# Block-sparse attention with a routed expert layer: the second pair's chunk 0 last, V's tiles loaded as needed, K in 1536-byte pieces, early dispatch over six steps

## The chip, the cores and the metric

The kernel runs on one core of one Trainium2 chip. Times are microseconds on the device. The median of 3 runs of the kernel before is 666.29 us (665.82 to 667.43). A profile is one execution of the program taken by the hardware profiler. Its times count from the first instruction, and "span" is the time to the last one.

The engines' names in the profile: PE is TensorE's matrix multiplication and PEld its loading of weights, DVE is VectorE, ACT is ScalarE, POOL is GpSimd, SP is SyncE, which only issues DMA here. PEq, DVEq and the like are sequencers. L511 is line 511 of the kernel before.

## The reference

There are two stages. The first is BigBird attention: 4 sequences of 768 tokens, 8 heads of width 64, float32. The keys are split into blocks of 32 tokens. A query block sees its own block and the two next to it, the first and the last block, and three sampled ones; the first and last query block see everything.

```python
scores = scale * np.matmul(q, k.transpose(0, 1, 3, 2))
mask = np.abs(blk_i - blk_j) <= window
mask = mask | (blk_i == 0) | (blk_j == 0) | (blk_i == n_blocks - 1) | (blk_j == n_blocks - 1)
for qb in range(n_blocks):
    for kb in sampled_blocks[qb]:
        mask[qb * block:(qb + 1) * block, kb * block:(kb + 1) * block] = True
scores = np.where(mask, scores, -1000000000.0)
attn = softmax(scores)                 # over the keys
attn_out = np.matmul(attn, v)
```

The second stage takes the 3072 attention rows of width 512 as `x`, sends each to one of 8 experts by the cosine of the row and the expert's embedding, and runs that expert's two layers:

```python
logits = xn @ en.T / tau               # rows of x and of expert_emb at unit length
expert_idx = np.argmax(logits, axis=1)
for e in range(8):
    mask = expert_idx == e
    h = np.maximum(x[mask] @ w1[e], 0.0)          # 512 to 1024
    out[mask] = gate_w[mask, None] * (h @ w2[e])  # 1024 to 512
```

## The kernel before

**Chunks and steps.** A sequence is cut into 6 chunks of 128 tokens, shifted by one block, so that chunk 0 holds the last block and the first three, and with them the sequence's two global query blocks. Two sequences form a pair; a pair-chunk is the same chunk of both. The loop in `attention_fast` (L1308) runs 25 steps. `TURNS` (L56) gives the chunk of each step, `n`, and `place` (L384) its sequence and chunk number: `n` from 0 to 11 belong to the first pair, from 12 to 23 to the second, and chunk 0 comes first in each pair. In step `s` the chunk `now` gets its scores (`score_near`, `score_far`). The chunk of the step before, `last`, is weighted with V (`weigh_near`, `weigh_far`) and divided (`normalize`). The one before that, `past`, is turned (`turn_x`) and gives logits (`chunk_logits`). The queries of the chunk `after` are turned (`turn_q`) and its sampled keys copied together (`gather_k`, one third on DVE and two thirds on POOL).

**Chunk 0** has half the near and half the far scores of another chunk. Its global rows need in addition `score_ends` (four times, one per pair of heads) and `weigh_ends`, which read all keys and all six V tiles of the sequence. They run in the step after the chunk's scores.

**Keys.** K comes in 16 groups (4 sequences by 4 pairs of heads). `load_k` (L412) fetches a group with two DMAs, each of 768 runs of 256 bytes, into one of 5 buffers. `turn_k` (L485) makes six transposes on PE into a PSUM tile of a ring of two, and one copy of 128 x 768 moves them to `kt`, on DVE for even groups and ACT for odd ones. Groups 8 to 15, of the second pair, are turned in steps 10, 11 and 12 (`turning`, L1303), and loaded in the steps that `keys_at` names.

**Values.** Six tiles `vt` hold V of a pair, and the second pair's overwrite the first's, in the steps that `values_at` names. `stack` (ACT) and `near_v` and `stack_ends` (POOL) copy what lies near from them. The sampled blocks come by `gather_v` from DRAM, 12 DMAs of 128 KB per pair-chunk (6 for chunk 0), into a ring of two tiles.

**SP's order.** All of these loads are issued by SP, one after the other, and a DMA whose buffer isn't free holds up all behind it. `fetch_all` (L464) puts the loads of a step between its gathers. The write of a finished pair-chunk's rows to `x_dram` (L808) is issued by SP too, at the start of a later step; the rows lie in three slots, so the write of pair-chunk `b` must land before `normalize` can begin pair-chunk `b + 3`.

**Routing and early dispatch.** `after_step` (L1211) hangs pieces of work on later steps, in their first half (0) or second half (1). For each pair-chunk it is `route`. Once the first two sequences are done, `dispatch_early` sorts their tokens into 5 expert tiles, mostly in small DVE operations. Its 18 calls run in steps 17, 18 and 19, three in each half. In step 20 the first tile's rows are gathered (`fetch_rows`), in steps 20 to 23 the first pieces of its weights are loaded.

**Experts.** `expert_tiles` works 23 tiles of 128 tokens, each with 4 MB of weights, in about 14 us of PE time. `dispatch_late` sorts the remaining tokens on DVE during the second tile, and `spread_slots` (L919) uses the constant `spread`. The first dispatch and the constants (`build_consts`, `build_tokens`) are set up in step 0.

Of the kernel before, what the change touches and what calls it, by code (L numbers as in the profile page):

```python
# [20 lines left out]
P = 128  # L21
# [32 lines left out]
DUO = 2  # L54
# [43 lines left out]
def build_consts(k):  # L98
    nc, pool = k.nc, k.const
    k.ones = pool.tile([P, P], F32, name="ones")  # L100
    nc.vector.memset(k.ones, 1.0)

    groups = k.ident.rearrange("p (g t) -> p g t", g=NG)
    k.spread = pool.tile([P, NG, NG, BLK], F32, name="spread")
    nc.vector.tensor_copy(out=k.spread, in_=groups.unsqueeze(2).broadcast_to([P, NG, NG, BLK]))
# [24 lines left out]
def build_tokens(k, shifted):  # L130

    nc, pool = k.nc, k.const
    tok = pool.tile([P, NT], I32, name="tok")
    pattern = [[-S * DUO, B // DUO], [-P, NC], [-S, DUO]] if shifted else [[-S, B], [-P, NC]]
    nc.gpsimd.iota(tok, pattern=pattern, base=N + BLK * shifted, channel_multiplier=-1)
    if shifted:
        first = tok.rearrange("p (a c i) -> p a c i", c=NC, i=DUO)[:, :, 0]
        nc.vector.tensor_scalar(out=first[0:BLK], in0=first[0:BLK], scalar1=-S, scalar2=None, op0=ALU.add)
    part = pool.tile([P, 2, NT], I32, name="tok_part")
    nc.vector.tensor_scalar(out=part[:, 0], in0=tok, scalar1=6, scalar2=None, op0=ALU.arith_shift_right)  # L140
    nc.vector.tensor_scalar(out=part[:, 1], in0=tok, scalar1=63, scalar2=None, op0=ALU.bitwise_and)
    k.tok = pool.tile([P, 2, NT], F32, name="tok_f")
    nc.vector.tensor_copy(out=k.tok, in_=part)
# [238 lines left out]


def place(n):  # L384

    a, rest = divmod(n, DUO * NC)
    c, i = divmod(rest, DUO)
    return DUO * a + i, c, i

# [13 lines left out]
def load_q(k, s, i=None):  # L403

    a, c = divmod(s, NC)
    if ("q", s) not in k.raw:
        k.raw["q", s] = k.ld.tile([P, DUO, H, D], F32, name="qraw", tag="qraw", bufs=2)
    t, src = in_pair(k.raw["q", s], i), of_seq(k.q, a, i)
    return [(t[rows], src[lo:lo + rows.stop - rows.start]) for rows, lo in pieces(c)]


def load_k(k, g):  # L412

    b, j = divmod(g, NPAIR)
    k.raw["k", g] = t = k.kld.tile([P, NC, 2, D], F32, name="kraw", tag="kraw", bufs=5)
    return [(t[:, :, h], k.k[b, 2 * j + h].rearrange("(c p) d -> p c d", p=P)) for h in range(2)]

# [12 lines left out]
def stack(k, s, i=None):  # L430

    st, c = k.st_ring[s % 2], s % NC
    for half in (1,) if c == 0 else (0, 1):
# [21 lines left out]
def gather_v(k, s, i=None):  # L455

    a, c = divmod(s, NC)
    t, src = k.vg_ring[s % 2], of_seq(k.v, a, i)
# [16 lines left out]
def near_v(k, s, some, i=None):  # L475

    c = s % NC
    for g in blocks_of(c):
# [6 lines left out]
def turn_k(k, g):  # L485
# [270 lines left out]
def route(k, b):  # L756
# [48 lines left out]
    a, c = divmod(b, NC)  # L805
    dram = k.x_dram[DUO * S * a:DUO * S * (a + 1), :].rearrange("(i s) w -> s i w", i=DUO)
# [404 lines left out]
def after_step(n, b):  # L1211
# [12 lines left out]
    if DUO * (b + 1) == EARLY * NC:  # L1224
        n.dispatching = partial(next, dispatch_early(n), None)
        plan += [(s + 4 + i // 6, i // 3 % 2, n.dispatching) for i in range(18)]
        s += 7
        plan += [(s, 0, partial(fetch_rows, n, 0))]
        n.first_weights = fetch_weights(n, 0, 0, 4)
        plan += [(s + i, 1, partial(next, n.first_weights)) for i in range(4)]  # L1230
        plan += [(s + 3, 1, partial(prepare, n, 0))]
    return [(min(when, NCH), part if when <= NCH else 1, what) for when, part, what in plan]


def attention_fast(n, ctx):
# [6 lines left out]
    n.ld, kv, n.qp, n.gp, n.pp = pool("ld", 1), pool("kv", 1), pool("qp", 2), pool("gp", 2), pool("pp", 2)  # L1242
    n.kld = brief = right.enter_context(n.tc.tile_pool(name="brief", bufs=1, side="right"))
    n.setup = setup.enter_context(n.tc.tile_pool(name="setup", bufs=1))
# [392 lines left out]
```

## Time and profile before

| | |
|---|---|
| median of 3 runs | 666.29 us |
| profiled execution's own time | 670.42 us |
| its span | 668.7 us |
| PE busy | 616.0 us, 92% |
| DVE, ACT, POOL busy | 233.5, 140.8, 243.8 us |
| attention, up to the first expert matmul | 302.8 us |
| DMA packets | 187,599; 148,008 of them under 512 bytes |
| mean granted PE clock | 0.955 |

The page cuts the span into 40 slices of 16.7 us; a digit is a busy share in tenths, and PEclk the granted clock in tenths. In a list of instructions the last bracket is the idle time of the engine before it and what ended that. A wait is given as its sum, the number of times and the longest. The chain of waits is followed back from the last instruction, so what stands in it set the end. A line of SP is the issue of a DMA[...].

### The profile page before, as it was taken

To read this page: it belongs to the slowest core of one execution; us is meant where nothing else is said; L and a number is where in the kernel's file an instruction comes from. 1 tells how busy PE (TensorE), PEld (TensorE's weight loads), DVE (VectorE), ACT (ScalarE), POOL (GpSimd) and SP (SyncE) were. 2 spreads that over 40 slices of the span, in tenths; PEclk is the share of its full clock that TensorE was granted. 3 is DMA by queue.
4 is the path that set the end of the run, shared out by engine and by line. 5 is a ranking of instruction groups with operands and counts; after the bars stand their busy time and mean duration, and the time that the engine had idled before them with its cause. 6 is when DMAs were issued, how large, how long until landed. Compare 5 with 4: busy or idle time off the path is not lost.

```text
span 668.7 us, 18349 instructions
## 1 busy us (share of the span) xinstructions
PE 616.0 (92%) x7496; PEld 480.2 (72%) x7496; DVE 233.5 (35%) x739; ACT 140.8 (21%) x285; POOL 243.8 (36%) x461
## 2 busy tenths in 40 slices
PE   6778996498799988999999999999999999999995
PEld 4667986387699887877777776675666765766773
DVE  3552472365334766642851122111121211121210
ACT  1533453154255534530000000000000001000000
POOL 1626264133362544521113433344333343433333
PEclk9897999699599977989999999999999999999999
DMA  9976999699857996839999999999899998999711
GB/s 170 178 145 143 140 165 182 158 170 190 156 90 98 158 141 102 190 131 314 391 396 398 407 397 398 365 321 330 313 411 392 408 374 310 406 399 397 287 49 32
DMA packets 187599, 170.57 MB, mean 255 GB/s; under 512 B 148008, under 2 KB 148136, under 8 KB 184690
## 3 DMA queue, kind: packets, MB, share of 16 engines
q1 hardware_dynamic: 180194, 155.35, 81.2%
q0 software_dynamic: 5216, 13.43, 5.6%
q8 instruction: 61, 1.00, 0.7%
q10 hardware_dynamic: 2096, 0.52, 0.5%
q14 instruction: 32, 0.26, 0.1%
HBM read 156.65 MB, written 12.90 MB: 254 GB/s over the span
## 4 chain that ended last, share of the span: by engine, by line
PE 82%; DVE 5%; SPq 5%; DMA 4%; issue 2%; ACT 1%; POOL 0%; DVEq 0%; POOLq 0%
PE hp L1142 25%; PE yp L1155 24%; PE av L622 8%; PE dps L567 5%; PE yp L710 4%; PE ac L542 3%; DMA kraw<-in_k_dram 3%; PE ac L545 2%; SPq L470 2%; PE xg_ps L506 2%; PE hp L1187 2%; PE yp L1207 2%; SPq L472 2%; PE xg_ps L699 2%; DVE xt L701 1%
## 5 line engine op out<-in xcount | busy, mean ns | idle before, releaser
L1142 PEld LDWEIGHTS hp<-xgt,w 128*128 128x128 f32 x1472 | 167.8, 192 | 10.3 <-issue 10.2
L1142 PE MATMUL hp<-xgt,w 128*128 128x128 f32 x1472 | 169.1, 275 | 0.0
L1155 PE MATMUL yp<-w,h 128*128 128x512 f32 x368 | 161.9, 592 | 0.0
L1155 PEld LDWEIGHTS yp<-w,h 128*128 128x128 f32 x368 | 68.1, 190 | 76.5 <-issue 72.0
L1066 POOL DMA_INDIRECT xg<-x_dram,quarter x88 | 89.2, 1014 | 32.3 <-issue 27.1
L1168 POOL DMA_INDIRECT out_dram<-y,slot_l x20 | 20.5, 1023 | 156.0 <-DVE y L1167 156.0
L1145 ACT ACTIVATE h<-hp 128x512 f32<-128x512 f32 x23 | 13.7, 597 | 284.0 <-PE hp L1142 254.9
L1149 DVE TENSOR_SCALAR h<-hp 128x512 f32<-128x512 f32 x23 | 15.9, 691 | 146.4 <-PE hp L1142 140.0
L482 POOL COPY vg<-vt 32x1040 f32<-32x1040 f32 (+1 forms) x45 | 43.2, 960 | 62.4 <-PE av L622 60.3
L524 POOL COPY kg<-kt 128x128 f32 x176 | 43.2, 291 | 57.4 <-ACT kt L495 45.3
L542 PE MATMUL ac<-qt,kt 128*64 128x128 f32 x352 | 48.7, 296 | 2.1 <-DVE qt L511 2.1
L567 PEld LDWEIGHTS dps<-qt,kg 128*64 128x64 f32 x1408 | 49.0, 143 | 1.6 <-POOL vg L482 1.5
L567 PE MATMUL dps<-qt,kg 128*64 128x64 f32 x1408 | 47.9, 228 | 1.3 <-DVE kg L524 1.3
L545 PE MATMUL ac<-qt,kt 128*64 128x256 f32 (+1 forms) x192 | 48.1, 399 | 0.8 <-ACT kt L498 0.8
L622 PE MATMUL av<-st,pac 128*64 128x65 f32 x704 | 33.0, 239 | 15.7 <-DVE x L799 15.7
L511 DVE COPY qt<-xg_ps 64x512 f32<-64x512 f32 x48 | 33.0, 688 | 40.9 <-PE xg_ps L506 40.6
L542 PEld LDWEIGHTS ac<-qt,kt 128*64 128x64 f32 x352 | 43.2, 152 | 3.1 <-ACT st L434 1.9
L1167 DVE TENSOR_SCALAR y<-yp,gate 128x512 f32<-128x512 f32 x20 | 15.0, 751 | 84.9 <-PE yp L1155 72.8
L622 PEld LDWEIGHTS av<-st,pac 128*64 128x64 f32 x704 | 27.5, 150 | 16.5 <-issue 16.0
L572 ACT ACTIVATE pd<-dps,bias 128x256 f32<-128x256 f32 x88 | 34.7, 474 | 17.2 <-PE dps L567 17.1
L622 PE MATMUL av<-vg,pd 128*32 128x65 f32 x1408 | 31.9, 234 | 0.8 <-issue 0.8
L622 PEld LDWEIGHTS av<-vg,pd 128*32 128x32 f32 x1408 | 24.2, 117 | 9.0 <-issue 8.6
(229 smaller groups left out, 631.0 us busy)
## 6 DMA issues: line engine op xcount, KB each, us to landing
w<-in_moe_w_dram SPq DMA_DIRECT2D x52, 2048.0 KB
vg<-in_v_dram SPq DMA_DIRECT2D x114, 128.0 KB
kraw<-in_k_dram SPq DMA_DIRECT2D x32, 192.0 KB
x_dram<-x SPq DMA_DIRECT2D x10, 516.0 KB
qraw<-in_q_dram SPq DMA_DIRECT2D x9, 512.0 KB
w<-in_moe_w_dram SPq DMA_DIRECT2D x8, 512.0 KB
vt<-in_v_dram SPq DMA_DIRECT2D x10, 256.0 KB
vt<-in_v_dram SPq DMA_DIRECT2D x5, 512.0 KB
```

Of the source, the lines that this page charges most:

```text
L482: k.nc.gpsimd.tensor_copy(out=k.vg_ring[s % 2][NRAND * BLK:P, g, which(i)], in_=k.vt[m][rows, which(i)])
L511: k.nc.vector.tensor_copy(out=t[rows, :, h], in_=ps[rows])
L524: copy(out=t[:, :, g, s * BLK:(s + 1) * BLK], in_=kt[:, :, bass.ds(shift, BLK)])
L542: nc.tensor.matmul(out[0:D, j, half], lhsT=kt[:, j, at:at + D], rhs=qt[:, j, :, D * half:D * (half + 1)], start=True, stop=True)
L545: nc.tensor.matmul(out[D:P, j, half:2].rearrange("p f h t -> p h f t"), lhsT=kt[:, j, S:S + D], rhs=qt[:, j, :, D * half:P].rearrange("p h ...
L567: nc.tensor.matmul(out[D * r:D * (r + 1), NG * j + g], lhsT=kg[:, j, g, D * r:D * (r + 1)], rhs=qt[:, j, :, cols], start=True, stop=True)
L572: nc.scalar.activation(e[:, :, g].rearrange("p j h t -> p j (h t)"), out.rearrange("p (j g) h t -> p j g (h t)", g=NG)[:, :, g], ACT.Exp, ...
L622: k.nc.tensor.matmul(av[lanes, h // NPAIR, h % NPAIR * P:h % NPAIR * P + D + 1], lhsT=lhsT, rhs=rhs, start=first[0], stop=last, skip_group ...
L710: k.nc.tensor.matmul(ps[:, 0:E], lhsT=xt[:, j], rhs=k.en[:, j, :], start=(j == 0), stop=(j == ND - 1))
L1066: k.nc.gpsimd.indirect_dma_start(out=x[:, g], out_offset=None, in_=quarters, in_offset=bass.IndirectOffsetOnAxis(ap=k.quarter[:, g, t:t + ...
L1142: nc.tensor.matmul(hp[:, f, :], lhsT=w1[:, d, (f0 + f) * P:(f0 + f + 1) * P], rhs=xt[:, d, :], start=(d == 0), stop=(d == ND - 1))
L1155: nc.tensor.matmul(yp, lhsT=h[:, f, :], rhs=w2[:, f, :], start=(f == 0), stop=(f == NF - 1))
```

## The change

There are four edits, and what they need around them.

1. `pair_chunk` replaces the division of a pair-chunk's number: the second pair works its chunks in the order 1, 2, 3, 4, 5, 0. Loads, gathers, `stack`, `near_v` and the writes use it, and the token numbers are made pair-chunk by pair-chunk (12 small iotas).
2. `load_k` takes six consecutive tokens per partition, so that a group is one DMA of 256 runs of 1536 bytes. `turn_k` transposes two tokens of one head at a time, and four copies of 64 x 384 put the tokens back in order; their output has a stride of six elements. There are 6 K buffers instead of 5. For the room, the tiles `pb` move to another pool, and `spread` is made in `dispatch_late`.
3. The second pair's K and V tiles get other steps. At the start, q of the second sequence goes ahead of its V tiles, and four of these go behind a gather.
4. The 18 calls of the early dispatch run in steps 16 to 21, one in the first half and two in the second; the first rows are gathered in step 22.

```diff
@@ build_tokens
     if shifted:
-        first = tok.rearrange("p (a c i) -> p a c i", c=NC, i=DUO)[:, :, 0]
-        nc.vector.tensor_scalar(out=first[0:BLK], in0=first[0:BLK], scalar1=-S, scalar2=None, op0=ALU.add)
+        for s in range(NS):
+            a, c = pair_chunk(s)
+            at = tok[:, DUO * s:DUO * (s + 1)]
+            nc.gpsimd.iota(at, pattern=[[-S, DUO]], base=N + BLK - S * DUO * a - P * c, channel_multiplier=-1)
+            if c == 0:
+                nc.vector.tensor_scalar(out=at[0:BLK], in0=at[0:BLK], scalar1=-S, scalar2=None, op0=ALU.add)
...
+def pair_chunk(s):
+
+    a, at = divmod(s, NC)
+    return a, at if a == 0 else (at + 1) % NC
...
 def load_k(k, g):
-    k.raw["k", g] = t = k.kld.tile([P, NC, 2, D], F32, name="kraw", tag="kraw", bufs=5)
-    return [(t[:, :, h], k.k[b, 2 * j + h].rearrange("(c p) d -> p c d", p=P)) for h in range(2)]
+    k.raw["k", g] = t = k.kld.tile([P, 2, NC, D], F32, name="kraw", tag="kraw", bufs=6)
+    return [(t.rearrange("p h c d -> p h (c d)"), k.k[b, 2 * j:2 * j + 2].rearrange("h (p c) d -> p h (c d)", p=P))]
@@ turn_k
-    for c in range(NC):
-        nc.tensor.transpose(ps[:, c // 3, c % 3 * P:(c % 3 + 1) * P], raw[:, c].rearrange("p h d -> p (h d)"), k.ident)
-    copy = nc.scalar.copy if g % 2 else nc.vector.tensor_copy
-    copy(out=kt[:, j, 0:S].rearrange("p (w t) -> p w t", w=2), in_=ps[:, :, 0:3 * P])
+    for h in range(2):
+        for m in range(NC // 2):
+            nc.tensor.transpose(ps[:, h, m * P:(m + 1) * P], raw[:, h, 2 * m:2 * m + 2].rearrange("p e d -> p (e d)"),
+                                k.ident)
+    for h in range(2):
+        to = kt[D * h:D * (h + 1), j, 0:S].rearrange("r (p m e) -> r e m p", m=NC // 2, e=2)
+        for e in range(2):
+            copy = nc.vector.tensor_copy if e == h else nc.scalar.copy
+            copy(out=to[:, e], in_=ps[D * e:D * (e + 1), h, 0:3 * P].rearrange("r (m p) -> r m p", m=NC // 2))
@@ dispatch_late
+    k.spread = p.tile([P, NG, NG, BLK], F32, name="spread")
+    nc.vector.tensor_copy(out=k.spread, in_=k.ident.rearrange("p (g t) -> p g t", g=NG).unsqueeze(2).broadcast_to(
+        [P, NG, NG, BLK]))
@@ after_step
-        plan += [(s + 4 + i // 6, i // 3 % 2, n.dispatching) for i in range(18)]
-        s += 7
-        plan += [(s, 0, partial(fetch_rows, n, 0))]
+        plan += [(s + 3 + i // 3, int(i % 3 > 0), n.dispatching) for i in range(18)]
+        plan += [(s + 9, 0, partial(fetch_rows, n, 0))]
         n.first_weights = fetch_weights(n, 0, 0, 4)
-        plan += [(s + i, 1, partial(next, n.first_weights)) for i in range(4)]
-        plan += [(s + 3, 1, partial(prepare, n, 0))]
+        plan += [(s + 7 + i, 1, partial(next, n.first_weights)) for i in range(4)]
+        plan += [(s + 10, 1, partial(prepare, n, 0))]
@@ attention_fast
-    n.pb_ring = [brief.tile([P, NC, 2, D], F32, name=f"pb{i}") for i in range(2)]
+    n.pb_ring = [n.pp.tile([P, NC, 2, D], F32, name=f"pb{i}", tag=f"pb{i}", bufs=1) for i in range(2)]
...
-    for g in range(5):
+    for g in range(NPAIR):
         fetch_all(n, (), load_k(n, g))
     for m in range(2):
         fetch_all(n, (), load_v(n, 0, m, 0))
+    for g in range(NPAIR, 6):
+        fetch_all(n, (), load_k(n, g))
...
-        if g + 5 < 2 * NPAIR:
-            fetch_all(n, (), load_k(n, g + 5))
-    fetch_all(n, gather_v(n, 1, 0), load_q(n, 0, 1))
-    for m in range(NC):
+        if g + 6 < 2 * NPAIR:
+            fetch_all(n, (), load_k(n, g + 6))
+    fetch_all(n, gather_v(n, 1, 0), load_q(n, 0, 1) + load_q(n, 1, 1))
+    for m in range(2):
         fetch_all(n, (), load_v(n, 0, m, 1))
-    fetch_all(n, gather_v(n, 0, 1), load_q(n, 1, 1))
+    fetch_all(n, gather_v(n, 0, 1), [])
+    for m in range(2, NC):
+        fetch_all(n, (), load_v(n, 0, m, 1))
     fetch_all(n, gather_v(n, 1, 1), [])
...
-    keys_at = {4: (8,), 5: (9,), 6: (10,), 7: (11,), 8: (12,), 10: (13, 14), 11: (15,)}
-    values_at = {4: (0,), 5: (1,), 6: (2,), 8: (3,), 9: (4,), 10: (5,)}
+    keys_at = {3: (8,), 4: (9,), 5: (10,), 6: (11,), 7: (12,), 8: (13,), 10: (14, 15)}
+    values_at = {7: (0,), 8: (1,), 9: (2,), 11: (3,), 13: (4,), 15: (5,)}
```

More of the change, by code (lines that the diff above doesn't have):

```diff
@@ L103, in build_consts @@
     groups = k.ident.rearrange("p (g t) -> p g t", g=NG)
-    k.spread = pool.tile([P, NG, NG, BLK], F32, name="spread")
-    nc.vector.tensor_copy(out=k.spread, in_=groups.unsqueeze(2).broadcast_to([P, NG, NG, BLK]))
     k.mine = pool.tile([P, NG], F32, name="mine")
@@ L133, in build_tokens @@
     tok = pool.tile([P, NT], I32, name="tok")
-    pattern = [[-S * DUO, B // DUO], [-P, NC], [-S, DUO]] if shifted else [[-S, B], [-P, NC]]
-    nc.gpsimd.iota(tok, pattern=pattern, base=N + BLK * shifted, channel_multiplier=-1)
     if shifted:
-        first = tok.rearrange("p (a c i) -> p a c i", c=NC, i=DUO)[:, :, 0]
-        nc.vector.tensor_scalar(out=first[0:BLK], in0=first[0:BLK], scalar1=-S, scalar2=None, op0=ALU.add)
+        for s in range(NS):
[4 more added lines that the diff above has]
+                nc.vector.tensor_scalar(out=at[0:BLK], in0=at[0:BLK], scalar1=-S, scalar2=None, op0=ALU.add)
+    else:
+        nc.gpsimd.iota(tok, pattern=[[-S, B], [-P, NC]], base=N, channel_multiplier=-1)
     part = pool.tile([P, 2, NT], I32, name="tok_part")
@@ L381, in shifts @@
     return k.shift[key]
+def pair_chunk(s):
+    a, at = divmod(s, NC)
+    return a, at if a == 0 else (at + 1) % NC
 def place(n):
-    a, rest = divmod(n, DUO * NC)
-    c, i = divmod(rest, DUO)
-    return DUO * a + i, c, i
+    a, c = pair_chunk(n // DUO)
+    return DUO * a + n % DUO, c, n % DUO
 def of_seq(src, a, i=None):
@@ L403, in load_q @@
 def load_q(k, s, i=None):
-    a, c = divmod(s, NC)
+    a, c = pair_chunk(s)
     if ("q", s) not in k.raw:
@@ L430, in stack @@
 def stack(k, s, i=None):
-    st, c = k.st_ring[s % 2], s % NC
+    st, (_, c) = k.st_ring[s % 2], pair_chunk(s)
     for half in (1,) if c == 0 else (0, 1):
@@ L455, in gather_v @@
 def gather_v(k, s, i=None):
-    a, c = divmod(s, NC)
+    a, c = pair_chunk(s)
     t, src = k.vg_ring[s % 2], of_seq(k.v, a, i)
@@ L475, in near_v @@
 def near_v(k, s, some, i=None):
-    c = s % NC
+    _, c = pair_chunk(s)
     for g in blocks_of(c):
@@ L804, in route @@
         return
-    a, c = divmod(b, NC)
+    a, c = pair_chunk(b)
     dram = k.x_dram[DUO * S * a:DUO * S * (a + 1), :].rearrange("(i s) w -> s i w", i=DUO)
@@ L1242, in attention_fast @@
     n.ld, kv, n.qp, n.gp, n.pp = pool("ld", 1), pool("kv", 1), pool("qp", 2), pool("gp", 2), pool("pp", 2)
-    n.kld = brief = right.enter_context(n.tc.tile_pool(name="brief", bufs=1, side="right"))
+    n.kld = right.enter_context(n.tc.tile_pool(name="brief", bufs=1, side="right"))
     n.setup = setup.enter_context(n.tc.tile_pool(name="setup", bufs=1))
```

## The prediction

> **What bounds the kernel now.** I read first the slices of the page, then the busy time by stretch, then the chain of waits, and last the queues in order of time inside the stretches that lose. A step is one turn of the attention loop; I find its end by the eight logits matmuls (L710), one group per step.
>
> The slices: TensorE is full in the second half (the experts), but holds 4, 6 and 7 in the first, with its clock down.
>
> ```profile
> PE   6778996498799988999999999999999999999995
> PEclk9897999699599977989999999999999999999999
> DMA  9976999699857996839999999999899998999711
> ```
>
> The same by stage. The columns are length, then busy us of PE, PEld, DVE, ACT, POOL, then granted clock, DMA share and GB/s.
>
> ```profile
> 0.00:66.30 66.30, 49.84 (x800) 41.27 (x800) 26.95 (x92) 22.93 (x44) 28.32 (x86) 0.92 0.82 159
> 99.50:132.60 33.10, 17.93 (x403) 16.22 (x401) 10.40 (x39) 8.71 (x19) 9.81 (x28) 0.79 0.90 172
> 140.90:180.00 39.10, 33.15 (x613) 29.25 (x615) 19.13 (x57) 14.19 (x32) 9.66 (x23) 0.84 0.98 173
> 180.00:209.50 29.50, 29.50 (x707) 27.34 (x707) 10.78 (x40) 13.95 (x25) 13.41 (x35) 0.92 0.53 81
> 226.40:270.10 43.70, 39.09 (x817) 35.96 (x813) 29.77 (x113) 17.88 (x38) 22.21 (x56) 0.84 0.84 127
> 278.40:302.80 24.40, 22.63 (x511) 20.11 (x511) 10.96 (x42) 8.93 (x21) 4.06 (x9) 0.93 0.56 166
> ```
>
> Rows: start to mid step 3; steps 7–8; 10–12; 13–14; 17–20; 22–24. An undisturbed step (4, 5, 6, 9) lasts 8.3 us. Steps 7–8 take 33.1 instead of 16.6, and 17–20 take 43.7 instead of 33.2. Steps 13–14 are full: there the second pair's chunk 0 does its global rows, with the DMA half idle.
>
> What ends each loss stands in the chain, in the waits, and in the engines' own order:
>
> ```profile
> 48.70 4.72 DMA qraw<-in_q_dram
> 121.04 4.34 DMA x_dram<-x
> 159.81 5.77 DMA kraw<-in_k_dram
> 168.55 3.83 DMA kraw<-in_k_dram
> ...
> DVE x L686 <- DMA x_dram<-x: 17.3, 1, 17.3
> ...
> 126.33 1.14 PE L622 MATMUL av<-st,pac 128*64 128x65 f32 x16 [14.98 <-DVE x L799]
> ...
> 232.41 0.66 PE L506 MATMUL xg_ps<-ident,qraw 128*128 128x128 f32 x4 [0.74 <-DVE xt L701]
> 242.28 0.75 PE L506 MATMUL xg_ps<-ident,qraw 128*128 128x128 f32 x4 [1.77 <-DVE xt L701]
> 255.43 0.66 PE L506 MATMUL xg_ps<-ident,qraw 128*128 128x128 f32 x4 [1.91 <-DVE xt L701]
> ```
>
> In step 7 `normalize` needs the x slot of pair-chunk 0 (three slots), whose write to DRAM stands in SP's order behind step 6's loads. Behind L686 on DVE stand the next key gathers, `xt` and `qt`, and TensorE waits for the accumulator that L686 reads. SP reached step 4's loads at 80.69 and, without a pause, the x write at 120.31: 27,136 packets of 256 bytes (counted from the loads' shapes), 1.46 ns each. So the transfers, not the arithmetic, set steps 7–12. In 17–20 the copy `xt` on DVE is late.
>
> [...] 256 bytes take 18–27 ns (median by stretch), 2,048 bytes 85, so 24 against about 11 bytes per ns in an engine; I take 1,536 bytes at 64 ns. [...] The trace agrees on the size (L542 272 ns or 476), and drops already after waits of 1.77 us, not after 0.74. [...] The new K copies write with a stride of six; no row here shows such a write.
>
> **The parts, against the profiled 668.7 us.**
>
> *Start and steps 0–3.* K falls from 24,576 packets to 16 x 256 = 4,096. For the first pair that is 12,288 x 1.46 ns = 17.9 us to 2,048 x 64 / 16 = 8.2. q of the second sequence now goes ahead of six V tiles (6,144 packets, 9 us). So the 3.34 us that TensorE waits for qraw at 53.55 goes, with the 6.8 us at half speed behind it (3.4): -6.7. K lands sooner, and DVE's chain to the first scores gains 1.2; the q wait of 0.68 at 37.6 goes. Against it stand the K copies. One copy per group (DVE 0.96 or ACT 0.80, in turn) becomes two on each engine of half the width. DVE: 384/0.96 + 157 = 0.56 us (L511 and L495 give that slope); ACT 0.49 (from L495's 0.80 for 768 and L550's 1.01 for 1,024). So 1.11 beside 0.98 per group instead of 0.44 on average: in step 1 four groups cost +1.3, +0.8 more with the copies' tail. Sum **-6.5**; range -3 to -9.
>
> *Steps 7–8.* Step 6's loads begin near 97.3 when SP is no longer behind: q 2,048 and V gathers 6,144 packets, 11.9 us, plus one K group 1.0. The x write is then issued near 110, lands near 114 (4.3 before), and TensorE, which can go on until 111.35, waits about 3.5 us instead of 15, with 1.2 at half speed. 16.5 lost becomes 4.7: **-11.8**; -8 to -16.5.
>
> *Steps 10–12.* 39.1 now. Three steps of 8.3 and eight groups of six transposes at 0.82 make 31.5; the later `qt`, behind up to three groups' copies of 1.11 on DVE, about 3.5. K 14 and 15 are issued a step earlier, at step 10. **-4.1**; +4 if strided writes take twice the time (0.4 more per copy), -7 at best.
>
> *Steps 13–14* become ordinary: 29.5 to 17.0, **-12.5**. DMA per two steps is then 11.9 + 1.4 (x) + 3.1 (one V tile) = 16.4 of 16.6 us: full, but each gather has 2.5 steps until its use. V tiles 2 to 5 are each wanted two steps after their issue, by ACT's `stack` and POOL's `near_v`, and the gathers of keys stand behind those on POOL.
>
> *Dispatch.* Its DVE work is 1.83 us in step 17, 3.02 in 18, 3.00 in 19; the idle was 0.74, 1.77, 1.91, so about 1.1 us per step is free. The new plan calls once in a step's first half and twice in its second, and what the second half issues runs on DVE at the head of the next step. By the calls' rows (a count and its sum 0.55; three adds of 0.3; tiles of experts 0.6, bases 0.75; two placements of 0.55, a shift of 0.5; splits 0.6 and 0.7; four of lanes 0.48; slots 0.65) that is 0.55, 0.9, 1.9, 1.65, 1.7 and 1.6 us in steps 16–21. Less 1.1 each, TensorE waits 2.5 us instead of 4.4, at most 0.8 at a time, and the 13.6 us at half speed that the clock's records show at 243–250 and 257–264 (6.8 lost) mostly go. That is -8.7; with one short drop of 3.4 us left, **-7**; -2 to -9. The first rows are then fetched at step 22 rather than 20, behind step 22's key gathers on POOL; they are used at the end of 23, 18 us later, where a late gather took 1 us to issue. If they took over 15, the first expert tile would wait. The weights' pieces stay in steps 20–23.
>
> *Tail.* 24.4 now. Step 22 halves its scores (8.3 to 6.5), 23 is like step 14 (14.2, 195.3 to 209.5) less the other half of its scores, 1.95, 24 the same less scores and q (9.7), plus 0.6 for its exponentials that nothing covers: 29.1, **+4.7**; +3 to +9.
>
> *At nothing:* eleven more iotas on POOL (0.2 each) lie in its 15.51 us wait for keys, 2.2 if that went; one more token subtraction on DVE (0.16) in its 6.92 us wait. `spread`'s copy (0.36) moves to where DVE has no gap (9.83 of 10 us busy at 330–340), but TensorE never waits there: **+0.4**. The pools' move and the sixth buffer change no wait that I can find: the last K is read at 173.4, the pool above it first written at 278.
>
> Sum -6.5 -11.8 -4.1 -12.5 -7 +4.7 +0.4 = -36.8. The profiled execution took 670.4, the median is 666.3: I subtract the same from it, **630 us** rounded. The experts' 366 us stay.
>
> **Rivals.** (a) The sum holds: 630, 622 to 638; chance 0.50. (b) Strided copies cost double and the clock still drops in the dispatch: +8 and +5, 643 (638 to 650); for it [...] that I can't say between 0.74 and 1.77 us where an idle wait begins to cost the clock; 0.22. (c) The x write lands before TensorE needs it, and no drop is left: -5, -5 and the outer ends elsewhere, 617 (610 to 622); for it a q and gather that took 10.0 us at 243; 0.13. (d) SP's order still holds the x write to where it was, and V loaded late stalls POOL: then the 11.8 and 4.1 are lost again, and four V tiles that stop the key gathers by some 2.5 us each (the longest K wait of before) take 10: 656 (650 to 664). Against it stand the 10,752 packets fewer ahead of the write, with only two K groups of 256 in their place; 0.09. (e) The other side: the K copies become the bound. If all 16 groups stand on the path, with two copies per engine each, they undo 36.8 us when a copy takes 0.56 + 36.8/32 = 1.7 us, three times its row. Then it ends above 668; [...] 0.05, with 0.01 for no change by luck.
>
> **How the numbers follow.** About 0.3% (2 us) is what a measurement of this kernel tells from no change. The likeliest is (a). The range takes (a), (b), and half of (c): 616 to 650, about 0.8. Faster by over 0.3%: all but (e) and no change, 0.94; within, 0.01; slower 0.05.
>
> **What would show it.** K's packets of 1,536 bytes at 60–70 ns; no wait of TensorE for qraw near 50; DVE's wait for the x write between 2 and 8 us; no K wait in steps 10–12; steps 13–14 at 8.3–8.7 and 23–24 at about 12 and 10; TensorE's waits for `xt` below 1.1 with the clock whole in 16–21; the K copies at 0.56 and 0.49. Wrong it would be if those copies take over 1 us, if V's tiles stop POOL or ACT in steps 11–17, or if the first expert tile waits for weights or rows.

## The result, and the profile after

The changed kernel is slower. Its median is 691.17 us (690.25 to 693.7) against 666.86 us of the kernel before in the same measurement: a ratio of 1.0366, 95% interval 1.0326 to 1.0405. The forecast was 630 us, with 616 to 650 as the range. The profiled execution took 691.25 us, with a span of 689.5 where before had 668.7, so what follows explains 20.8 us, where the medians lie 24.3 apart.

The slices of the page of the changed kernel, 17.2 us each:

```profile
PE   5493999696677999999999999999999999999996
PEclk9995999888678999999999999999999999999998
DMA  8972479999529999623999999999899998999811
```

Against the slices of before, the holes have moved. TensorE's second slice falls from 7 to 4, it has a new hole in the fourth (52 to 69 us) and a longer one in the tenth to thirteenth (155 to 224 us), and around these two the DMA has a hole as well (2 and 4, then 5 and 2): there the kernel isn't short of data. From 224 us on TensorE is full.

The busy time by stretch of the changed kernel (length, then busy us of PE, PEld, DVE, ACT, POOL, then clock, DMA share, GB/s): start to step 3, steps 8–9, 10–12, 17–20. A step ends here with the last of its logits matmuls.

```profile
0.00:88.70 88.70, 58.74 (x953) 49.13 (x954) 39.42 (x106) 35.72 (x59) 31.47 (x99) 0.90 0.67 139
123.10:149.70 26.60, 20.75 (x401) 18.81 (x402) 10.13 (x39) 8.84 (x19) 10.58 (x33) 0.81 1.01 182
149.70:205.10 55.40, 40.67 (x653) 36.63 (x652) 26.33 (x67) 25.35 (x44) 10.09 (x21) 0.75 0.66 114
245.40:279.60 34.20, 32.60 (x803) 29.82 (x802) 25.76 (x106) 17.66 (x38) 19.82 (x57) 1.00 0.96 157
```

Steps 10–12 last 55.4 us with 14.7 of it idle on TensorE, the clock at 0.75 and the DMA share down from 0.98 to 0.66. Steps 17–20 have a full clock, which before they had not (0.84).

The same ends of steps, worked out from the traces of before and after, and of two kernels that the experiments explain: `e1` (the change with K as before) and `e6` (the change with one copy per group). In us; in brackets the difference to before.

| stretch | forecast | before | after | e1 | e6 |
|---|---|---|---|---|---|
| start to step 3 | -6.5 | 72.5 | 88.7 (+16.2) | 67.8 (-4.7) | 68.6 (-3.9) |
| 4–6 | 0 | 26.1 | 26.1 (0) | 26.1 (0) | 26.1 (0) |
| 7–9 | -11.8 | 41.4 | 34.9 (-6.5) | 36.9 (-4.5) | 32.1 (-9.3) |
| 10–12 | -4.1 | 38.6 | 55.4 (+16.8) | 38.5 (-0.1) | 39.8 (+1.2) |
| 13–16 | -12.5 | 46.9 | 40.3 (-6.6) | 33.5 (-13.4) | 34.5 (-12.4) |
| 17–20 | -7 | 43.7 | 34.2 (-9.5) | 34.1 (-9.6) | 34.1 (-9.6) |
| 21 | 0 | 8.3 | 8.8 (+0.5) | 8.8 (+0.5) | 8.8 (+0.5) |
| 22 to first expert matmul | +4.7 | 25.3 | 33.9 (+8.6) | 34.0 (+8.7) | 34.0 (+8.7) |
| experts | +0.4 | 365.9 | 367.2 (+1.3) | 368.9 (+3.0) | 367.2 (+1.3) |
| sum | -36.8 | 668.7 | 689.5 (+20.8) | 648.6 (-20.1) | 645.2 (-23.5) |

The two stretches in which K is turned (steps 0–1, 10–12) lose 33.0 us; by the forecast they gain 10.6. What happens in them is seen in the engines' order in time, at the first groups of K:

```profile
11.45 0.83 DVE L507 COPY kt<-kps 64x384 f32<-64x384 f32 x1
12.32 1.66 ACT L507 COPY kt<-kps 64x384 f32<-64x384 f32 x2 [8.47 <-DVE kt L507]
14.01 1.70 DVE L507 COPY kt<-kps 64x384 f32<-64x384 f32 x2 [1.73 <-ACT kt L507]
14.94 1.51 PE L501 MATMUL kps<-ident,kraw 128*128 128x128 f32 x6 [2.47 <-issue]
15.74 1.67 ACT L507 COPY kt<-kps 64x384 f32<-64x384 f32 x2 [1.76 <-DVE kt L507]
```

A group's four copies run one after another, DVE, ACT, ACT, DVE, and each begins 0.03 to 0.04 us after the other engine's has ended. In the row of DVE's `x2` the first copy belongs to one group and the second to the next. The transposes of the third group begin 2.47 us late. The view names no releaser for that, but the last copy of the first group's tile ended just before them (14.01 + 0.83 = 14.84), and the ring has two tiles. The list of the tile `kps` of the changed kernel (minimum, median and maximum in ns), and the waits of the changed kernel (sum, times, longest):

```profile
L507 DVE COPY kt<-kps x32: 821/832/869, 11.5 to 206.3; 64x384 f32<-64x384 f32 x32
L507 ACT COPY kt<-kps x32: 820/826/862, 12.3 to 205.4; 64x384 f32<-64x384 f32 x32
```

```profile
DVE kt L507 <- ACT kt L507: 28.9, 16, 2.7
PE ac L554 <- DVE qt L523: 14.5, 4, 5.5
DVE x L698 <- DMA x_dram<-x: 8.1, 1, 8.1
```

A copy takes 0.83 us on either engine, not 0.56 and 0.49. Behind them on DVE stand `qt` and, on POOL and DVE, the key gathers. From 51.84 to 65.52 us the chain of waits of the changed kernel is made of the 16 copies of groups 4 to 7: 13.7 us in a row. In the kernel before, the same four groups' copies lie between 41.85 and 45.23, 3.4 us. TensorE's stops, out of its own order in time:

```profile
133.29 1.14 PE L634 MATMUL av<-st,pac 128*64 128x65 f32 x16 [5.65 <-DVE x L811]
165.95 0.44 PE L554 MATMUL ac<-qt,kt 128*64 128x128 f32 x1 [5.53 <-DVE qt L523]
210.57 0.45 PE L554 MATMUL ac<-qt,kt 128*64 128x128 f32 x1 [4.64 <-DVE qt L523]
269.17 0.65 PE L518 MATMUL xg_ps<-ident,qraw 128*128 128x128 f32 x4 [0.83 <-DVE xt L713]
```

Where before TensorE waited for K to arrive (159.81 and 168.55 in the chain of before), it now waits for queries that stand on DVE behind K's copies. The first of these lines is the x write's wait (14.98 before), the last the longest wait for `xt` in the dispatch (1.91 before).

### The profile page after: what moved, and what is told of

Same layout as the page of the kernel before. It is cut to its first block, busy times and chain, and to the rows that moved or that the text cites. A ratio compares the mean times of both kernels' runs of the same rounds, so it can differ in the third digit from the quotient of the medians.

```text
span 689.5 us, 18383 instructions
## 1 busy us (share of the span) xinstructions
PE 620.6 (90%) x7496; PEld 483.9 (70%) x7496; DVE 254.0 (37%) x764; ACT 162.1 (24%) x310; POOL 245.2 (36%) x472
## 4 chain that ended last, share of the span: by engine, by line
PE 76%; DVE 8%; ACT 5%; DMA 2%; issue 2%; SPq 1%; POOL 0%; DVEq 0%; POOLq 0%; ACTq 0%
PE hp L1157 23%; PE yp L1170 22%; PE av L634 7%; PE dps L579 5%; PE ac L554 3%; PE yp L722 3%; PE ac L557 3%; ACT kt L507 3%; DVE kt L507 2%; PE hp L1202 2%; PE yp L1222 2%; PE xg_ps L518 2%; DMA w<-in_moe_w_dram 2%; DVE xt L713 2%; PE xg_ps L711 1%
## 5 line engine op out<-in xcount | busy, mean ns | idle before, releaser
L1160 ACT ACTIVATE h<-hp 128x512 f32<-128x512 f32 x23 | 13.7, 597 | 284.1 <-PE hp L1157 240.4
L554 PE MATMUL ac<-qt,kt 128*64 128x128 f32 x352 | 52.1, 309 | 16.5 <-DVE qt L523 14.5
L554 PEld LDWEIGHTS ac<-qt,kt 128*64 128x64 f32 x352 | 46.1, 159 | 17.8 <-issue 15.7
L557 PE MATMUL ac<-qt,kt 128*64 128x256 f32 (+1 forms) x192 | 51.6, 422 | 3.2 <-ACT kt L510 3.2
L579 PEld LDWEIGHTS dps<-qt,kg 128*64 128x64 f32 x1408 | 50.7, 147 | 2.4 <-issue 2.4
L584 ACT ACTIVATE pd<-dps,bias 128x256 f32<-128x256 f32 x88 | 34.7, 475 | 20.2 <-PE dps L579 20.2
L507 DVE COPY kt<-kps 64x384 f32<-64x384 f32 x32 | 26.8, 838 | 29.3 <-ACT kt L507 28.9
L507 ACT COPY kt<-kps 64x384 f32<-64x384 f32 x32 | 26.6, 832 | 29.0 <-DVE kt L507 28.6
L501 PE MATMUL kps<-ident,kraw 128*128 128x128 f32 x96 | 17.7, 341 | 16.6 <-issue 16.6
```

The lines of the kernel that those rows point to most:

```text
L507: copy(out=to[:, e], in_=ps[D * e:D * (e + 1), h, 0:3 * P].rearrange("r (m p) -> r m p", m=NC // 2))
L554: nc.tensor.matmul(out[0:D, j, half], lhsT=kt[:, j, at:at + D], rhs=qt[:, j, :, D * half:D * (half + 1)], start=True, stop=True)
L557: nc.tensor.matmul(out[D:P, j, half:2].rearrange("p f h t -> p h f t"), lhsT=kt[:, j, S:S + D], rhs=qt[:, j, :, D * half:P].rearrange("p h ...
L579: nc.tensor.matmul(out[D * r:D * (r + 1), NG * j + g], lhsT=kg[:, j, g, D * r:D * (r + 1)], rhs=qt[:, j, :, cols], start=True, stop=True)
L584: nc.scalar.activation(e[:, :, g].rearrange("p j h t -> p j (h t)"), out.rearrange("p (j g) h t -> p j g (h t)", g=NG)[:, :, g], ACT.Exp, ...
```

## The experiments

Two causes can stand behind the copies: that they wait for one another, because both engines read one PSUM tile, and that their output has a stride of six elements (24 bytes). "Attention's end" is the first expert matmul in the profile: 302.8 us in the kernel before, 322.3 in the changed one. Each ratio is to the kernel before, run beside it.

**The other edits without K's.** `e1_k_old` is the changed kernel with `load_k` and `turn_k` as before (six buffers stay).

```diff
-    k.raw["k", g] = t = k.kld.tile([P, 2, NC, D], F32, name="kraw", tag="kraw", bufs=6)
+    k.raw["k", g] = t = k.kld.tile([P, NC, 2, D], F32, name="kraw", tag="kraw", bufs=6)
...
+    for c in range(NC):
+        nc.tensor.transpose(ps[:, c // 3, c % 3 * P:(c % 3 + 1) * P], raw[:, c].rearrange("p h d -> p (h d)"), k.ident)
+    copy = nc.scalar.copy if g % 2 else nc.vector.tensor_copy
+    copy(out=kt[:, j, 0:S].rearrange("p (w t) -> p w t", w=2), in_=ps[:, :, 0:3 * P])
```

> The changed kernel with K loaded and turned as before (two DMAs of 256-byte runs, one copy per group; six buffers stay), and everything else of the change kept. Theory 1 (the loss is the K copies: four per group, one after the other across DVE and ACT): about 655 us, since the steps in which K is turned lost some 36 us against before and the other steps gained. Theory 2 (the loss is the order: chunk 0 last, V late, the tail without cover): 685 us or more.

Measured: 650.34 us, ratio 0.9756 (0.9695 to 0.9818); attention ends at 279.7. So the other edits are worth some 16 us, and K's, in their company, cost 42.7 us of attention. Step 12 keeps its wait for K, from TensorE's order in time in `e1`:

```profile
164.01 1.51 PE L500 MATMUL kps<-ident,kraw 128*128 128x128 f32 x6 [4.62 <-DMA kraw<-in_k_dram]
```

**K's edit alone.** `e2_k_alone` is the kernel before with the new `load_k` (five buffers) and `turn_k`, the reverse of the diff above.

> The kernel before with only K's loading and turning changed (1536-byte runs, four strided copies per group; five buffers). Theory 1: slower than before, about 690 us: 19 us more in the first steps, about 15 in steps 10 to 13, less what the shorter DMA gives back. Theory 2: 660 us or less, because the loads get shorter and nothing else changes.

Measured: 701.44 us, ratio 1.0535 (1.0463 to 1.0607); attention ends at 332.8, 30.0 later than before. The loss is K's edit, with or without the rest.

**The order of the copies.** `e3_by_head` gives the two copies of one head to DVE and of the other to ACT, and `e7_by_group` all four copies of a group to one engine, the next group's to the other. In `e7` no copy of K waits for the other engine's copy of the same group.

```diff
@@ e3_by_head
-            copy = nc.vector.tensor_copy if e == h else nc.scalar.copy
+            copy = nc.scalar.copy if h else nc.vector.tensor_copy
@@ e7_by_group
-            copy = nc.vector.tensor_copy if e == h else nc.scalar.copy
+            copy = nc.scalar.copy if g % 2 else nc.vector.tensor_copy
```

> The changed kernel with the four copies of a group given out by head: both of head 0 on DVE, both of head 1 on ACT, so that no copy waits for one on the other engine; number, size and stride stay. Theory 1a (waits between the two engines): a group takes 1.7 us instead of 3.43, 16 groups 28 us less at most, about 665 us. Theory 1b (only the time per copy counts, 0.83 instead of 0.56): the same as the change, 689 us within 4.

> The changed kernel with all four copies of a group on one engine, DVE for even groups and ACT for odd; number, size and stride stay. The kernel giving the copies by head still had ACT's copies of a group wait for DVE's of the same group, although they write other rows. Theory A (the wait comes from two engines reading one PSUM tile): now no copy waits for a copy on the other engine, a group takes 3.4 us on its engine but two run at once, so about 670 us, like the kernel that gave them by head. Theory B (the wait comes from writing one kt tile): the waits between DVE and ACT stay, and the time is near the change's 690.

Measured: `e3` 669.99 us, ratio 1.0052 (1.0029 to 1.0075), attention's end 306.0; `e7` 673.8 us, ratio 1.011 (1.0019 to 1.0202), attention's end 302.1. Number, size and stride of the copies are those of the changed kernel. First `e3`, then `e7`, in order of time:

```profile
11.36 3.38 DVE L507 COPY kt<-kps 64x384 f32<-64x384 f32 x4
13.13 3.38 ACT L507 COPY kt<-kps 64x384 f32<-64x384 f32 x4 [9.29 <-DVE kt L507]
```

```profile
11.33 3.37 DVE L507 COPY kt<-kps 64x384 f32<-64x384 f32 x4
12.41 3.34 ACT L507 COPY kt<-kps 64x384 f32<-64x384 f32 x4 [8.56 <-PE kps L501]
```

In `e3` ACT still waits for both of DVE's copies of its group, but then runs beside DVE's copies of the next group. In `e7` its first copy waits for TensorE alone. Either way a group costs 1.7 us of the two engines instead of 3.4, and attention ends 16.3 or 20.2 us sooner. A profile is one run, and that of `e3` was the slowest of its twenty; by the medians `e3` and `e7` are 21.2 and 17.4 us faster than the changed kernel. So the order alone makes about half of K's 42.7 us.

**Do two engines wait because of the tile they read?** `e12_split` puts the question to the kernel before: each group's one copy is cut into two of 128 x 384, contiguous, which read the two halves of the tile (banks 0 and 1 in the expectation).

```diff
-    copy = nc.scalar.copy if g % 2 else nc.vector.tensor_copy
-    copy(out=kt[:, j, 0:S].rearrange("p (w t) -> p w t", w=2), in_=ps[:, :, 0:3 * P])
+    for w, copy in enumerate((nc.vector.tensor_copy, nc.scalar.copy)):
+        copy(out=kt[:, j, w * 3 * P:(w + 1) * 3 * P], in_=ps[:, w, 0:3 * P])
```

> The kernel before with each group's one copy cut in two of 128 x 384, bank 0 of the PSUM tile on DVE and bank 1 on ACT: other columns of kt, other banks, no stride. Theory A (two engines that read one PSUM tile are put one after the other): ACT's copy starts only when DVE's has ended, a group takes 0.56 + 0.49 = 1.05 us instead of 0.96 or 0.80, and the kernel is some 0 to 6 us slower than before. Rival (they run at once): copies of a group overlap, and the kernel is the same or up to 4 us faster.

Measured: 668.31 us, ratio 0.9999 (0.9967 to 1.0031). The first group of `e12`, and after it two groups of the kernel before, in order of time:

```profile
10.04 0.56 DVE L495 COPY kt<-kps 128x384 f32<-128x384 f32 x1
10.64 0.48 ACT L495 COPY kt<-kps 128x384 f32<-128x384 f32 x1 [6.71 <-DVE kt L495]
```

```profile
41.85 0.96 DVE L495 COPY kt<-kps 128x768 f32<-128x768 f32 x1
42.48 0.78 ACT L495 COPY kt<-kps 128x768 f32<-128x768 f32 x1
```

Both engines write the same `kt` in either pair. They run beside each other where their PSUM tiles differ, and one after the other where they share a tile. So the output is not what holds them; the shared tile is. The view names DVE's copy as what ended ACT's wait of 6.71 us, and ACT's copy begins 0.04 us after DVE's has ended (10.64 after 10.04 + 0.56). In these runs the wait goes by whole tiles: in `e12` the two copies read different halves, in the changed kernel each of the four reads its own quarter of the tile, and they wait all the same (16 waits of DVE for ACT there, 28.9 us). Whether two engines could read one tile without it, no run here shows, and a tile for each half was not tried.

**The stride.** `e5_contig` lets the changed kernel's four copies write contiguous stretches of 384. It computes attention over keys in a permuted order, so that rows and routing are others and more expert tiles run; of its time only attention's end can be compared.

```diff
-        to = kt[D * h:D * (h + 1), j, 0:S].rearrange("r (p m e) -> r e m p", m=NC // 2, e=2)
+        to = kt[D * h:D * (h + 1), j, 0:S].rearrange("r (e m p) -> r e m p", m=NC // 2, e=2)
```

> The changed kernel with the copies writing contiguous stretches of 384 (keys come out in another order, so this kernel computes attention over permuted keys); engines and number as in the change, but the stretches no longer interleave. Theory 1a: no waits between the engines, a group about 1.1 us, and about 655 us. Stride: a copy takes 0.56 on DVE and 0.49 on ACT if the stride of six elements is what makes it 0.83; it stays at 0.83 if the move to other partitions or the half width does.

Measured: attention's end 304.9; in all 712.45 us, ratio 1.0668 (1.0596 to 1.0739). The tile `kps` in `e5`:

```profile
L507 DVE COPY kt<-kps x32: 549/555/561, 11.6 to 189.1; 64x384 f32<-64x384 f32 x32
L507 ACT COPY kt<-kps x32: 471/474/477, 12.2 to 188.6; 64x384 f32<-64x384 f32 x32
```

These are nearly the 0.56 and 0.49 of the forecast, and attention still ends 2.1 us later than before, because the four copies still take turns. Right durations alone would not have made it right.

**One copy per group, with and without the stride.** `e4_one_copy` multiplies each head's tokens by the identity into the head's own 64 rows, so that one copy of 128 x 768 per group does, on the two engines in turn, and writes with the stride of six. `e6_one_copy_tok` is the same, but its copy goes through the tokens in order: it writes consecutive elements and reads PSUM with a stride of 512 bytes.

```diff
+    for c in range(NC):
+        for h in range(2):
+            nc.tensor.matmul(ps[D * h:D * (h + 1), c // 3, c % 3 * P:(c % 3 + 1) * P], lhsT=raw[:, h, c], rhs=k.ident,
+                             start=True, stop=True)
+    copy = nc.scalar.copy if g % 2 else nc.vector.tensor_copy
@@ e4_one_copy
+    copy(out=kt[:, j, 0:S].rearrange("r (p w m) -> r w m p", w=2, m=NC // 2),
+         in_=ps[:, :, 0:3 * P].rearrange("r w (m p) -> r w m p", m=NC // 2))
@@ e6_one_copy_tok
+    copy(out=kt[:, j, 0:S].rearrange("r (p w m) -> r p w m", w=2, m=NC // 2),
+         in_=ps[:, :, 0:3 * P].rearrange("r w (m p) -> r p w m", m=NC // 2))
```

> The changed kernel with K's new loading kept, but each token of each head turned by itself into the rows of that head (12 half-width multiplications by the identity instead of 6 transposes), so that one copy of 128 x 768 per group does it, DVE and ACT in turn, writing with the stride of six. The stride's price from the runs [...] gives 1.5 us per copy. Theory 1: about 640 us, less than the 650 of the kernel with the old K, since the shorter K loads now pay. If the stride alone is enough to eat the gain of the loads: 650 or more.

> The same with the copy's order turned round: it writes consecutive elements and reads PSUM with a stride of 128 elements. If the stride costs on the writing side only, a copy takes 0.96 us on DVE and 0.80 on ACT, and the kernel some 2 to 5 us less than the one before; if a stride in PSUM costs as much or more, 1.5 us or more per copy and no gain.

Measured: `e4` 652.49 us, ratio 0.9798 (0.9708 to 0.9889), attention's end 282.8; `e6` 650.02 us, ratio 0.9756 (0.9667 to 0.9845), attention's end 278.0. The copies in `e4`, then in `e6`:

```profile
L504 DVE COPY kt<-kps x8: 1521/1535/1577, 12.2 to 164.7; 128x768 f32<-128x768 f32 x8
L504 ACT COPY kt<-kps x8: 1494/1531/1595, 13.5 to 166.6; 128x768 f32<-128x768 f32 x8
```

```profile
L504 DVE COPY kt<-kps x8: 957/958/958, 12.6 to 162.9; 128x768 f32<-128x768 f32 x8
L504 ACT COPY kt<-kps x8: 798/798/802, 14.9 to 164.2; 128x768 f32<-128x768 f32 x8
```

From `e7` to `e4` the copies of a group go from 3.37 us on one engine to 1.53, which is 19.3 us of attention; without the stride 4.8 more. So the 44.3 us between the changed kernel and `e6` are 20.2 of copies that take turns, 19.3 of four half-width copies for one, and 4.8 of the stride in that one. These parts depend on the order in which they are taken away; the stride is also in the 19.3. They are of single profiles; by the medians the three steps are 17.4, 21.3 and 2.5 us.

The forecast of 640 us for `e4` counted on a gain from the shorter K loads. None shows: `e6` has them and copies as fast as before, but twelve multiplications per group instead of six transposes, and it takes 650.02 us where `e1`, with K as before, took 650.34.

**The order of the chunks and V's steps.** `e8_no_order` is `e1` with the pair-chunks, `keys_at` and `values_at` of before, and five K buffers: q ahead of V and the spread dispatch are left.

```diff
-    return a, at if a == 0 else (at + 1) % NC
+    return a, at
...
+    keys_at = {4: (8,), 5: (9,), 6: (10,), 7: (11,), 8: (12,), 10: (13, 14), 11: (15,)}
+    values_at = {4: (0,), 5: (1,), 6: (2,), 8: (3,), 9: (4,), 10: (5,)}
```

> The changed kernel with the old K, and besides with the chunks of the second pair in their old order and K and V of the second pair loaded in their old steps: what is left of the change is the early dispatch over six steps and the order of the first loads. My reading of the steps: 4 us less at the start, 9.5 less in steps 17 to 20, so about 653 to 655 us; order and V together then are worth only 4 us or so, because the tail gives back 9.7 of the 13.5 that steps 13 to 15 gain. If the order is worth what the prediction said (12.5 less 4.7, and 11.8 for the x write): 662 us or more.

Measured: 656.36 us, ratio 0.9833 (0.9743 to 0.9924); attention's end 289.4, 9.7 later than `e1`. Steps 17–20 take 34 us as in `e1`, and the start 68.0, so the dispatch and q's place do their work alone. The medians lie 6.0 us apart, but the intervals of `e8` and `e1` overlap; that the order is worth anything rests on the two profiles. Since `keys_at`, `values_at` and the sixth buffer go with it, the order by itself is not separated.

**Who holds the x write?** Rows of finished pair-chunks are written by SP, in its order. `e9_act_write` is `e6` with these writes issued by ACT during attention, `e10_no_order_k` is `e9` with chunk order and `values_at` of before, and `e11_before_act` the kernel before with ACT's writes.

```diff
-        nc.sync.dma_start(out=dram[lo:lo + rows.stop - rows.start], in_=x[rows].rearrange("p i e w -> p i (e w)"))
+        (nc.scalar if k.attending else nc.sync).dma_start(out=dram[lo:lo + rows.stop - rows.start], in_=x[rows].rearrange("p i e w -> p i (e w)"))
```

> The kernel with one copy per group in token order and, besides, the write of a finished pair-chunk's rows issued by ACT instead of SP while attention runs. In that kernel step 8 still takes 15.5 us where 8.3 would do, with 4.9 us of waiting for the x slot. If SP's order holds the write up: the wait goes, about 643 us. If the DMA engines' backlog does: the write lands as late as now, 650 us.

> The kernel of the run before with the chunks of the second pair in their old order, and V's second tiles in their old steps. With the old K the order and V together were worth 7.8 us of span. If that holds with the new K and without the wait for the x slot: about 651 us against 643. If most of it was relief of the DMA queues, which the new K gives too: within 4 us of the run before.

> The kernel before with only the write of the rows issued by ACT instead of SP while attention runs. If SP's order holds it up: step 8 falls from 24.8 us to about 10, and the kernel to about 652 us, or 657 if the waits for K in steps 10 to 12 grow by what the loads now lack in time. If the backlog does: 666 us, no change.

Measured: `e9` 652.93 us, ratio 0.9768 (0.9684 to 0.9851); `e10` 652.73 us, ratio 0.9755 (0.967 to 0.984); `e11` 677.49 us, ratio 1.0148 (1.0059 to 1.0237). The wait for the x slot has gone in all three. TensorE's own longest waits in `e11`:

```profile
PE av L622 <- DMA vg<-in_v_dram: 15.7, 9, 7.5
PE kps L493 <- DMA kraw<-in_k_dram: 10.6, 5, 5.3
```

In the kernel before, the K wait of this list was 6.3 us, and there is none for V's gathers. What makes loads late here stands among SP's own waits (first line) and in the busy times of two stretches of `e11` (the last three columns are the clock, the DMA share and GB/s):

```profile
SPq L468 <- DMA x_dram<-x: 17.0, 2, 11.9
80.00:90.00 10.00, 9.81 (x238) 9.13 (x236) 7.84 (x27) 6.15 (x14) 7.74 (x22) 1.00 1.23 169
90.00:102.00 12.00, 10.70 (x274) 9.71 (x269) 7.76 (x32) 6.53 (x16) 7.84 (x24) 1.00 0.30 55
```

SP stood for 11.9 us, up to 102.02, in front of the load of a V tile, until a write that ACT had issued at 99.96 had landed. Meanwhile the DMA share fell to 0.30. Why that load waits for that write is not shown. In all, SP waits for writes of x 59.7 us in nine waits in `e11`, and its gathers alone 45.4 us in eight waits in `e9`; in no kernel whose SP issues these writes does it wait for one. So ACT's queue took the write out of SP's order, but put SP's loads behind the write, and TensorE waits for V's gathers in these runs (15.7 us in `e11`, 8.5 us in `e9`). That is neither of the two causes that the forecasts set against each other. Whether SP's order or the supply of the DMA engines bounds steps 7–12 stays open, and that `e10` is no slower than `e9` (both carry this wait) says little about the order of the chunks without it.

No run beats `e1` and `e6` by more than the intervals. These two beat both kernels: 650 us, against 667 and 691.

## Why the prediction was wrong

**The step that failed** is the sentence on the K copies under *Start and steps 0–3*: one copy per group "becomes two on each engine of half the width", so "1.11 beside 0.98 per group". Two things in it were wrong. The word "beside": the four copies take turns, because both engines read one PSUM tile. And the price of a copy: 0.56 and 0.49 were of contiguous copies, and with the stride of six it is 0.832 and 0.826. Without the stride the same copies take 0.555 and 0.474 (`e5`), so it makes them 1.50 times as long on DVE and 1.74 on ACT. Twice the time for a strided copy, in *Steps 10–12* and rival (b), was an estimate that no row of the profile before could test. A group thus takes 13.68/4 = 3.42 us of the path, where 1.11 was assumed, and 16 groups at 2.31 more are 37 us, the size of the whole forecast gain. Measured against `e6`, the copies cost 44.3 us.

That is the point at which rival (e) decides: its "1.7 us" per copy, two copies in a row per engine, is 3.4 us per group. It was given 0.05, and no row of the profile before shows a copy of three times its price. None was needed: one and a half times the price on DVE, 1.74 times on ACT, and two engines in turn give 3.1 times (3.42 us against 1.11). The rival had the right place and the wrong mechanism for it, and so 0.05 was too little. The falsifier was as blind: "over 1 us" per copy asks for the duration of a copy and not whether two overlap.

Point by point:

- *Start and steps 0–3*, forecast -6.5, was +16.2. First scores of the sampled keys (`dps`) begin at 29.65 instead of 20.74, and groups 4 to 7 cost 13.7 us instead of 3.4. The wait for qraw near 50 us did go. In `e1` the clock's drop behind it went too (a score matmul of 128 x 128 takes 0.27 us at 53.20, where before it took 0.42 from 57.2 to 60.4), and the stretch gains 4.7; in the changed kernel another drop stands in its place, at the K copies (clock 0.58 from 51.7 to 68.9). Even with the copies mended K's fewer packets bring nothing at the start (`e6` gains 3.9). One part of it is TensorE: for twice four groups its records take 7.78 and 5.69 us in `e6`, where before had 5.85 and 3.06.
- *Steps 7–8*, forecast -11.8, was -6.5. SP began step 6's loads at 113.48 and reached the x write at 126.33, 12.9 us later, as worked out (11.9 and 1.0). But the write's second piece, issued 0.7 us after the first, took 5.3 us to land and not 4.3 (127.06 in the chain of waits, before 121.04), so TensorE waited 5.65 instead of 3.5, and the half speed behind it (clock 0.70 from 133 to 150 us) cost some 4 us by estimate, not 1.2: the three steps lost 10.0, and 5.85 of that is idle time. Mechanism right, two terms too small.
- *Steps 10–12*, forecast -4.1, was +16.8. No wait for K is left, as said. In its place stand the waits for `qt` of 5.53 and 2.79 us behind K's copies and two of 3.70 and 2.71 that end when a tile comes free, and the clock at 0.75. Without K's edit the stretch gains nothing (`e1`, -0.1): K comes late as before. With one copy per group it doesn't either (`e6`, +1.2).
- *Steps 13–14*, forecast -12.5: -13.4 in `e1` and -12.4 in `e6`, over 13–16. In the changed kernel the last K copies reach into step 13 (`qt` 4.64 us late), and -6.6 is left.
- *Dispatch*, forecast -7, was -9.5, and much the same in every kernel with it (34.0 to 34.5 us) but `e9` (36.6). `xt` is late by 0.42 and 0.83 us, and the clock is whole (1.00) from 226 to 280 us. The short drop that was kept back didn't come. But the reading behind it, that the clock drops after 1.77 us and not after 0.74, doesn't hold in general: see the last section.
- *Tail*, forecast +4.7, was +8.6. Step 23 lasts 12.4 us (12.3 by the sum); step 24 lasts 12.7, where 10.3 were worked out, with 1.35 us of TensorE's wait for the rows `x` in front of a near weighting; where the other 1.1 us come from stays open. The wait of 0.59 for exponentials falls in step 23. The first expert matmul follows the last logits 2.1 us later and not 0.8, since near and end weightings of chunk 0 are still to be done.
- *At nothing*: for the experts +0.4 was forecast, for `spread`; they took +1.3, of which 0.9 is one wait for weights. No pool or iota shows up in a wait.
- *K's packets* took 67 ns (median) in the first 50 us, near the 64 taken, and 91 to 120 by stretches of about 50 us later. 1,536 bytes in 67 ns are 23 bytes per ns; the 256-byte packets of before, at 18 to 27 ns, had 9.5 to 14. But bytes per packet were not what K lacked: `e6` has the long packets and takes 650.02 us, `e1` the short ones and 650.34.

Had the copies cost what was assumed, `e6` is about where it would have ended: -23.5 us, at 650 us. So of the 57.6 us between forecast and profile (-36.8 and +20.8) 44.3 are the copies, and the rest of the forecast was some 13 us too hopeful as well, most of it in steps 7–12 and the tail.

## What to carry to other kernels

Before a copy is split between two engines, look whether the two read one tile: in this program they then take turns, and the price is the sum of both (0.56 and then 0.48 us in `e12`, 3.42 us per group in the changed kernel). Price a copy by its access on both sides: of the copies of 128 x 768 here, the one that reads PSUM with a stride of 512 bytes takes what a contiguous one takes (0.958 us on DVE, 0.798 on ACT, `e6`), the one that writes SBUF with a stride of 24 bytes 1.535 and 1.531 us (`e4`). Set the wait for a transfer against what is done to the data to shorten it: K's longer packets came with twelve multiplications per group instead of six transposes, and brought nothing (650.02 us in `e6`, 650.34 in `e1`). And a transfer moved to another engine's queue isn't free of the old one: once ACT issued the writes of x, SP waited 59.7 us for them (`e11`). Look for what the old queue then waits for.

## What the runs showed of the hardware that was not expected

- A stride of 24 bytes in the output of a float32 copy from PSUM to SBUF cost 50% on DVE (0.555 us in `e5`, 0.832 in the changed kernel, for 64 x 384) and 74% on ACT (0.474 and 0.826). On the two engines the strided copy took nearly the same time.
- A stride of 512 bytes in what is read from PSUM cost a copy nothing in `e6`: 0.958 and 0.798 us for 128 x 768, the times of the kernel before for contiguous reads (0.958 and 0.798).
- In these two traces the length of a wait alone doesn't tell whether TensorE's clock falls to 0.50; one setting of it lasts 3.41 us or a multiple of that (at half 3.41 to 17.07 us; the record's end cuts the last), so the stretches below are of 3.4 us. In the kernel before it fell after waits of 1.77 and 1.91 us, but also at 297.33, 0.6 us into a wait of 0.74, the longest since 264 us. In the changed kernel it held through 0.83 us (269.17) and 1.35 us (311.61); there TensorE was busy 2.06 of the 3.4 us that end with the wait, and in the kernel before 2.54 of the 3.4 us up to the drop. The last wait and two stretches of before, then the wait and two stretches of the changed kernel (the clock is the third number from the end):

```profile
297.48 1.14 PE L622 MATMUL av<-st,pac 128*64 128x65 f32 x16 [0.74 <-DVE x L799]
293.90:297.30 3.40, 2.54 (x36) 2.12 (x35) 1.03 (x4) 0.17 (x1) 0.00 (x1) 1.00 0.43 132
297.30:300.70 3.40, 3.22 (x64) 2.81 (x68) 2.15 (x9) 0.72 (x2) 0.00 (x0) 0.50 0.41 155
```

```profile
311.61 0.45 PE L634 MATMUL av<-st,pac 128*64 128x65 f32 x8 [1.35 <-DVE x L698]
308.20:311.60 3.40, 2.06 (x54) 1.77 (x50) 1.75 (x6) 0.10 (x1) 0.00 (x0) 1.00 0.02 5
311.60:315.00 3.40, 3.39 (x78) 2.88 (x79) 1.41 (x7) 1.85 (x4) 0.00 (x0) 1.00 0.41 155
```
